# An mLSTM cell and a multiplicative feed-forward block on one core: four PSUM banks taken in another order, one product kept for the end, and unit 0's k and q loaded and turned ahead of the gates

## The chip, the core and the metric

The kernel runs on one NeuronCore of a Trainium2 chip. The metric is the device time of one execution in microseconds (us). A core has five engines that run their own queues in order: TensorE (PE, matrix products), VectorE (DVE), ScalarE (ACT), GpSimd (POOL) and SyncE (SP), which here only issues transfers. Sixteen DMA engines move the data.

## What is computed

Two blocks follow each other. The first is an mLSTM cell with stabilised exponential gates over 768 steps, for 4 batches of 8 heads with 40 channels. The second takes its output as 3072 tokens of 320 channels through a multiplicative feed-forward block:

```python
for t in range(S):
    m_new = np.maximum(f_gate[:, :, t] + m, i_gate[:, :, t])
    f_stab = np.exp(f_gate[:, :, t] + m - m_new)
    i_stab = np.exp(i_gate[:, :, t] - m_new)
    m = m_new
    C = f_stab * C + i_stab * outer(vt, kt)
    n = f_stab * n + i_stab * kt
    y[:, :, t] = sigmoid(o_gate) * (C @ qt) / np.maximum(np.abs(n @ qt), 1.0)
x = y.transpose(0, 2, 1, 3).reshape(B * S, H * D)
a = x @ w1; b = x @ w2            # 320 -> 1024
out = (a * b @ w3) @ w_out        # 1024 -> 1024 -> 320
```

The inputs q, k, v and the gates are float32, the four weights double precision (two 32-bit words each).

## The kernel before, in words

The sequence is cut into 24 units (`NU`): unit n is 128 time steps of one batch with its 8 heads, taken as two chunks of 64. The cell is computed in chunks, with matrix products within a chunk and a state carried between chunks. The feed-forward block works on six groups of four units. Since (ab w3) w_out = ab (w3 w_out), the kernel first forms `w3o` = w3 w_out (the `wp` products) and then needs per group only a, b, their product `ab` and `po` = ab w3o.

A main loop of 32 steps (lines 709 to 802) interleaves everything. In step s the loop issues the loads of unit s+2 (`load` at line 125: k, q, v, and `load_o`), weighs v of unit s on GpSimd, turns k and q of unit s on TensorE and copies them out on ScalarE (`turn`, up to unit 9), runs the cell products of units s and s-1 (`quarter_work`), and as many feed-forward products as the lists `n_up`, `n_seven` and `n_down` say. Two weight pieces or so are made float32 in each of the first steps (`convert`: ScalarE scales the high words, VectorE does four passes). The matmuls stand on TensorE in exactly the order in which they are written, by a chain of dependences (`in_order`, line 84). Ahead of the loop stands a front: loads in a fixed order (lines 459 to 474), the gates, the masks of unit 0, and the first two conversions.

*Gates.* The gates lie as 96 rows by 256 columns, a third of the sequence for each of 32 heads. Line 514 scans f into F (running sums in chunks of 64), line 517 scans the maximum into U, line 519 carries the running maximum M over the chunks; `before` is M ahead of each chunk. From these come U (minus the stabilised maximum, relative) and a, which is needed with tokens on partitions: `gate_cols` transposes it on TensorE (`pg`) and ScalarE copies it to aT. VectorE forms U in three passes, GpSimd forms a in two beside it. `dec` and `pick` become the decay of the state, `w` the weights of v (wT), and `weights(0)` makes the masks of unit 0: TensorE spreads U over the partitions (`ub`), ScalarE takes eight exps into `pw`, GpSimd clears what lies above the diagonal.

*PSUM.* There are eight banks. Four belong to the pool `ps_m`, handed out in rotation by `mps` (line 77), and four to the two cell tiles. When the cell is finished (after step 24, line 781), the cell tiles are closed and a pool `ps_x` of four banks takes their place. `mps` keeps a list `banks` of pools, takes the first and puts it at the end, so that with two pools in the list the tiles come from them in turn.

*Groups 3 to 5.* They are done with seven products in place of eight (`up_by_seven`, Strassen's scheme in Winograd's form), one piece per step in steps 19 to 30. A piece has four parts: `shared` (p15 and p67: 16 matmuls as the trace counts, named p there), `single` (pa, pb), `left` (the last rows of x, then VectorE's sums into a_sb and ab) and `product` (VectorE, line 676: ab times a_sb). Between `shared` and `single`, after step 24, stands a `po` product of an earlier group (`ffn_out`, line 680: 8 products over f, 16 matmuls in the trace; ScalarE copies the result to o_sb and sends it out). The last step, 31, runs four such products, of the group that step 30 finished. The eight f of one such product need all pieces of the group.

Of the kernel before, what the change touches and what calls it, by code (L numbers as in the profile page):

```python
# [10 lines left out]
AF = mybir.ActivationFunctionType  # L11
OP = mybir.AluOpType
# [4 lines left out]
def kernel(  # L17
# [26 lines left out]
    nc = tc.nc  # L44

    B, H, S, D = q.shape
    L = 64
# [25 lines left out]
    banks = [ps_m]  # L73
# [28 lines left out]
    NB, NBQ = 4, 3  # L102
# [19 lines left out]
        c, b = divmod(n, B)  # L122
        return src[b, :, c * P:(c + 1) * P, :].rearrange("h p d -> p h d")

    def load(n):
        for dst, src in ((kbuf[n % NB][:, :, 0:D], k), (qbuf[n % NBQ][:, :, 0:D], q), (vbuf[n % NB][:, :, 0:D], v)):
            if src is not q or n < N_DVE:
                nc.sync.dma_start(out=dst, in_=rows(src, n))  # L128

# [73 lines left out]
    def fetch(kind, i, part):  # L203

        if kind == "w12":
            c0 = part * CW
            if i < 2 * KF:
                wt, src = ((w1, w1_d), (w2, w2_d))[i // KF]
                ko = i % KF
                dst, pieces = wt[:, ko, c0:c0 + CW], [(every, src[ko * 128:(ko + 1) * 128, cols(c0, CW)])]  # L210
            else:
                dst, pieces = wr[:, c0:c0 + CW], [(slice(j * REM, (j + 1) * REM), src[KF * P:DM, cols(c0, CW)])
                                                  for j, src in enumerate((w1_d, w2_d))]
        elif kind == "wo":
            dst, pieces = wo[:, i, :], [(square, wo_d[j * CQ + i * 32:j * CQ + (i + 1) * 32, :])
                                        for j, square in enumerate(squares)]
        else:
            dst, pieces = None, [(square, w3_d[i * 128 + part * 64:i * 128 + (part + 1) * 64, cols(j * CQ, CQ)]
                                  .rearrange("(m r) n -> r m n", m=2)) for j, square in enumerate(squares)]
        pend.append((dst, raw_tile(dst.shape[-1] if dst is not None else CW, pieces), i, part))  # L220
# [5 lines left out]
    def scale_next():  # L226
        scaled.append(pend.pop(0))
        scale(scaled[-1][1])
# [56 lines left out]
    def turn(n):  # L285


        if n >= N_DVE:
            for src, dst, name in zip(turned_in[n % 2], (kT_t, qT_t), ("kT", "qT")):
                dst[n] = sb.tile([128, NP, P], FP, name=name, tag=name)  # L290
                done = nc.vector.transpose(out=dst[n].rearrange("i p (r f) -> i p f r", f=4),
                                           in_=src[:, 32:TB].rearrange("i (p f d) -> i p f d", p=NP, f=4)[:, :, :, 0:32])
            return done
        for src, dst, name in ((kbuf[n % NB], kT_t, "kT"), (qbuf[n % NBQ], qT_t, "qT")):
            pt = mps([128, NP, P], "pt")
            for p in range(NP):
                transpose(pt[:, p, :], src[:, 2 * p:2 * p + 2, :].rearrange("p a b -> p (a b)"))
            dst[n] = sb.tile([128, NP, P], FP, name=name, tag=name)
            nc.scalar.copy(out=dst[n], in_=pt)  # L299
# [162 lines left out]
        nc.scalar.dma_start(out=a[r], in_=i_gate.rearrange("b h s -> (b h) s")[:, cs])  # L462

    w3o_words = w3o.rearrange("p f d -> p (f d)").bitcast(U32).rearrange("p (n two) -> p n two", two=2)
    fetch("w12", 0, 0)
    fetch("w12", 1, 0)
    load(0)
    load_o(0)
    fetch("w12", 2, 0)
    idle += [w3o_words[:, i * CW:(i + 1) * CW] for i in range(2)]  # L470
# [39 lines left out]
    V = nc.vector  # L510
# [10 lines left out]
        if i + 1 < GR:  # L521
            V.tensor_copy(out=M[third[i + 1], 0:1], in_=M[r, GC:GC + 1])
    before = M[:, 0:GC].unsqueeze(2).to_broadcast([RG, GC, L])
    V.tensor_tensor(out=U3, in0=U3, in1=before, op=OP.subtract)
    nc.gpsimd.tensor_tensor(out=a3, in0=a3, in1=before, op=OP.subtract)
    V.tensor_tensor(out=U, in0=U, in1=F, op=OP.max)
    nc.gpsimd.tensor_tensor(out=a, in0=a, in1=F, op=OP.subtract)
    V.tensor_tensor(out=U, in0=F, in1=U, op=OP.subtract)
    for i, r in enumerate(third):
        nc.sync.dma_start(out=U_d[i * GC:(i + 1) * GC].rearrange("c r t -> r c t"), in_=U3[r])  # L530
    def gate_cols(src, dst, copy):
        pg = mps([P, GC // 2, GR, BH], "pg")
        for c in range(GC // 2):
            transpose(pg[:, c].rearrange("p g r -> p (g r)"), src[:, c * P:(c + 1) * P], RG)
        for c in range(GC // 2):
            copy(out=dst.rearrange("p (g c) r -> p c g r", g=GR)[:, c], in_=pg[:, c])

    scale_next()
    nc.scalar.activation(out=dec, in_=U3[:, :, L - 1], func=AF.Exp)
    gate_cols(a, aT, nc.scalar.copy)  # L540
    V.tensor_tensor(out=w3d, in0=a3, in1=U3[:, :, L - 1:L].to_broadcast([RG, GC, L]), op=OP.add)
    scale_next()
    convert()
# [6 lines left out]
    pd = mps([P, B * NP * NT], "pd")  # L550
    for x in range(2):
        mm(pd[halves[x]], odd[:, x].to_broadcast([RG, L]), pick.rearrange("p j g c -> p (j g c)"))
    turn(0)
    gate_cols(w, wT, nc.scalar.copy)
    nc.scalar.copy(out=decay.rearrange("p j c -> p (j c)"), in_=pd)
    nc.scalar.activation(out=g, in_=U, func=AF.Exp)
# [141 lines left out]
    sevens = [(gr, f) for gr in range(3, NG) for f in range(FH)]  # L698
    n_up = [0] * 4 + [1] * 2 + [2] * 11 + [0] * 15
    n_seven = [0] * 19 + [1] * 12 + [0]  # L700
    n_down = [0] * 17 + [2] * 6 + [1] * 8 + [4]
    w12 = [("w12", i, part) for part in range(2) for i in range(2 * KF + 1)]
    todo = w12[KF * 2 + 1:] + [("wo", i, 0) for i in range(FO)] + [("w3", ko, part) for ko in range(FO) for part in range(2)]
    n_cvt = [2, 1, 1, 1, 2, 2, 3, 3, 3] + [2] * 7
# [4 lines left out]
    for s in range(len(n_up)):  # L709
        if B <= s + 3 < NU:  # L710
            load_u(s + 3)
        if s + 2 < NU:
            load(s + 2)
            load_o(s + 2)
        if 0 < s < B - 1:
            weights(s + 1)
            out_gate(s)
        if s < NU:
            weighted(s)
            if s >= B:  # L720
                decayed(state[s % B][1], state[s % B][0], s, 0)
            if 0 < s < N_DVE:
                turn(s)
        if NY <= s - 2 < NU:
            send(s - 2)
        elif 0 <= s - 2 < NY:
            twice(s - 2)
        if NY <= s - 2 < NU:
            get_back(s - 2)
        while turned < min(s - 2, NY):  # L730
            x_trans(turned)
            turned += 1
        fold()
        seven = None
        if n_seven[s]:
            seven = up_by_seven(*sevens.pop(0), (lambda i: cell[i // 2][:, i % 2].rearrange("p (i t) -> p i t", i=2)) if s <= NU else
                                lambda i: mps([128, 2, TH], "p67" if i < 2 else "p15"))
            if s <= NU:
                seven[0]()
            seven[1]()  # L740
        if seven and s <= NU:
            ffn_out([downs.pop(0) for _ in range(n_down[s])], [cell[1][:, i, 0:DM] for i in range(2)])
        else:
            for _ in range(n_down[s]):
                ffn_out([downs.pop(0)])
        if seven and s > NU:
            seven[0]()
        now = [ups.pop(0) for _ in range(n_up[s])]
        open_ups = [up(*x) for x in now]
        if len(now) == 1 and turned == s - 2 < NY:  # L750
            x_trans(turned)
            turned += 1

        def rest():
            for x in open_ups:
                up_rest(*x)
            if seven:
                seven[2]()

        gated = None  # L760
        if s <= NU:
            gated = quarter_work(s, rest)
        else:
            rest()
        with tc.issue_after(gated.ins) if gated else nullcontext():
            if seven:
                seven[3]()
            if NY <= s - 2 < NU:
                x_turn(s - 2)
            if N_DVE <= s + 1 < NU:  # L770
                gated = turn(s + 1)
            if s in (16, 17):
                weight_sums(s - 16)
            if s - 2 in range(4 * GT - 1, NU, GT):
                token_sums((s - 2) // GT)
        if s == 0:
            gate_cols(g, gT, nc.scalar.copy)
            out_gate(0)
            scale_next()
            weights(1)  # L780
        if s == NU:
            cell_psum.close()
            banks.append(ctx.enter_context(tc.tile_pool(name="ps_x", bufs=4, space=bass.MemoryType.PSUM)))
        if B - 1 <= s < NU:
            if s + 1 < NU:
                weights(s + 1)
            out_gate(s)
        with tc.issue_after(gated.ins) if N_DVE <= s + 1 < NU else nullcontext():
            for _ in range(n_cvt[s] if s < len(n_cvt) else 0):
                convert()  # L790
                converted += 1
        if s >= ahead:
            while pend and len(scaled) < 2:
                scale_next()
        if N_DVE <= s + 2 < NU:
            load_turned(s + 2)
        while todo and fetched < converted + (2 if s < 2 else 3 if s < ahead - 1 else 4):
            fetch(*todo.pop(0))
            fetched += 1
        if s + 1 == pinned:  # L800
            for ins in keep_order(front):
                behind.enter_context(tc.issue_after(ins))
# [30 lines left out]
```

## Time and profile before

Three runs took 451.50, 451.76 and 454.91 us; the median is 451.76. The profiled execution took 451.65 us with a span of 449.8 us and a mean granted TensorE clock of 0.984.

| what | value |
|---|---|
| TensorE busy | 428.3 us, 95% of the span |
| VectorE busy | 342.5 us, 76% |
| ScalarE, GpSimd busy | 134.5 us (30%), 84.1 us (19%) |
| moved by DMA | 52.71 MB, 117 GB/s over the span |
| chain that ended last | TensorE 75%, DMA 8%, SyncE's issue 8%, VectorE 4% |
| L92 pa from xT, w: 240 matmuls | 62.3 us |
| L92 po from w3o, ab: 224 matmuls | 62.2 us |
| L309 idle of GpSimd before it | 183.2 us |

How to read it: a row of the profile names the source line, the engine, the operation, what it writes and reads, how often it ran, and its busy time; behind it stands how long the engine stood idle just before and what ended the wait. A line can be that of a helper: every matmul has line 92 and every transpose line 95, so they are told apart by their tiles. The busy share of TensorE is an average: its matmuls overlap, and the chain of waits tells better where the time is set. Idle time of an engine that is not the bottleneck costs nothing, such as GpSimd's above.

### The profile page before, as it was taken

What the parts mean: (1) busy time and instruction counts of PE and PEld (TensorE: products, weight loads), DVE (VectorE), ACT (ScalarE), POOL (GpSimd) and SP (SyncE); (2) the same over time, 40 slices, a digit from 0 to 9 for tenths busy, and PEclk for the clock granted to TensorE, in tenths of its full rate; (3) what the DMA queues carried; (4) which work ended last, traced back from release to release, by engine and by line L of the source; (5) the groups of instructions that cost most, each with busy time, mean ns of one, the idle gap of its engine ahead of it and who ended that gap; (6) DMA issues with size and microseconds to landing.
All of it is one profiled execution on the core that took longest, in us unless ns stands there. A gap on an engine that the chain in (4) does not pass through costs nothing.

```text
span 449.8 us, 12909 instructions
## 1 busy us (share of the span) xinstructions
PE 428.3 (95%) x5271; PEld 339.4 (75%) x5271; DVE 342.5 (76%) x703; ACT 134.5 (30%) x376; POOL 84.1 (19%) x156
## 2 busy tenths in 40 slices
PE   2998989999999999999999999999999899999997
PEld 2887778787778878887877877878777677777764
DVE  6699599999998988898868859759698856444530
ACT  3754454434533244133302320312210111101100
POOL 5353133333211220222022203202100000000000
PEclk9995899999999999999999999999999999999999
DMA  8999979797979786687466467264121110000001
GB/s 184 186 166 185 201 156 172 138 197 172 202 188 204 156 172 164 162 163 148 97 111 141 106 133 148 72 131 101 42 50 33 38 32 17 15 16 15 16 15 44
DMA packets 136554, 52.71 MB, mean 117 GB/s; under 512 B 109936, under 2 KB 127536, under 8 KB 136496
## 3 DMA queue, kind: packets, MB, share of 16 engines
q1 hardware_dynamic: 132896, 47.87, 53.1%
q10 hardware_dynamic: 3600, 4.03, 2.6%
q8 instruction: 41, 0.67, 0.7%
q14 instruction: 17, 0.14, 0.1%
HBM read 46.07 MB, written 5.80 MB: 115 GB/s over the span
## 4 chain that ended last, share of the span: by engine, by line
PE 75%; DMA 8%; SPq 8%; DVE 4%; issue 2%; ACT 1%; POOL 0%; DVEq 0%; ACTq 0%
PE cell L92 21%; PE pa L92 16%; PE po L92 13%; PE pb L92 10%; PE wp L92 7%; PE p L92 5%; SPq L173 4%; DMA kbuf<-in_k_dram 3%; DMA raw<-in_moe_w_dram 2%; DMA raw<-in_moe_w_out_dram 2%; SPq L128 2%; DMA q_all<-in_q_dram 1%; PE pt L95 1%; SPq L137 1%; PE px L95 1%
## 5 line engine op out<-in xcount | busy, mean ns | idle before, releaser
L92 PE MATMUL pa<-xT,w 128*128 128x256 f32 x240 | 62.3, 392 | 0.8 <-ACT xT L440 0.8
L92 PE MATMUL po<-w3o,ab 128*128 128x320 f32 x224 | 62.2, 434 | 0.8 <-DVE ab L676 0.8
L92 PEld LDWEIGHTS po<-w3o,ab 128*128 128x128 f32 x224 | 42.4, 190 | 18.2 <-DVE ab L676 1.3
L309 POOL TENSOR_TENSOR state<-state,decay 128x164 f32<-128x164 f32 x40 | 19.7, 492 | 183.2 <-DVE den L390 180.8
L92 PEld LDWEIGHTS pa<-xT,w 128*128 128x128 f32 x240 | 45.7, 195 | 9.1 <-ACT xT L440 1.6
L92 PE MATMUL pb<-xT,w 128*128 128x256 f32 x192 | 45.6, 381 | 0.8 <-ACT kT L299 0.8
L633 DVE SCALAR_TENSOR_TENSOR a_sb<-pa,wo 128x512 f32<-128x512 f32 x12 | 8.3, 692 | 48.9 <-PE pa L92 48.9
L282 POOL TENSOR_SCALAR_AFFINE_SELECT pw<-pw 64x512 f32<-64x512 f32 x48 | 35.0, 729 | 52.6 <-ACT pw L280 51.0
L92 PE MATMUL cell<-w3o,ab 128*128 128x320 f32 x160 | 44.0, 432 | 0.0
L92 PEld LDWEIGHTS pb<-xT,w 128*128 128x128 f32 x192 | 36.6, 191 | 6.4 <-ACT kT L299 1.5
L280 ACT ACTIVATE pw<-pw,aT 128x64 f32<-128x64 f32 x160 | 40.3, 336 | 2.9 <-ACT o_sb L688 2.9
L92 PEld LDWEIGHTS cell<-w3o,ab 128*128 128x128 f32 x160 | 30.5, 190 | 12.0
L585 ACT ACTIVATE a_sb<-pa 128x512 f32<-128x512 f32 x24 | 14.3, 597 | 76.8 <-PE pb L92 76.8
L92 PE MATMUL pa<-xT,wr 64*64 64x256 f32 x384 | 36.8, 386 | 0.0
L92 PE MATMUL wp<-wo,w3T 128*128 128x320 f32 x128 | 35.9, 433 | 0.5 <-DVE ab L586 0.5
L92 PE MATMUL pb<-xT,wr 64*64 64x256 f32 x384 | 36.2, 380 | 0.0
L382 DVE TENSOR_TENSOR h<-cell,h 64x164 f32<-64x164 f32 x96 | 31.2, 325 | 1.8
L92 PEld LDWEIGHTS wp<-wo,w3T 128*128 128x128 f32 x128 | 23.7, 190 | 9.6 <-DVE ab L586 0.7
L92 PEld LDWEIGHTS pa<-xT,wr 64*64 64x64 f32 x384 | 19.0, 133 | 14.4 <-issue 8.4
L688 ACT COPY o_sb<-po 128x320 f32<-128x320 f32 x14 | 6.0, 425 | 68.4 <-PE po L92 64.5
L586 DVE TENSOR_TENSOR ab<-pb,a_sb 128x512 f32<-128x512 f32 x24 | 16.1, 686 | 12.2 <-ACT a_sb L585 12.2
L178 ACT ACTIVATE raw<-raw 128x512 f32<-128x512 f32 (+1 forms) x32 | 19.1, 627 | 12.4 <-DMA raw<-in_moe_w_dram 11.2
(124 smaller groups left out, 749.8 us busy)
## 6 DMA issues: line engine op xcount, KB each, us to landing
raw<-in_moe_w_dram SPq DMA_DIRECT2D x64, 128.0 KB, 3.1
pw<-U_d SPq DMA_DIRECT2D x40, 128.0 KB, 4.1
kbuf<-in_k_dram SPq DMA_DIRECT2D x24, 160.0 KB, 4.3
vbuf<-in_v_dram SPq DMA_DIRECT2D x24, 160.0 KB, 4.9
o_in<-in_o_gate_dram SPq DMA_DIRECT2D x24, 160.0 KB, 4.4
out_dram<-o_sb ACTq DMA_DIRECT2D x24, 160.0 KB, 1.8
raw<-in_moe_w_dram SPq DMA_DIRECT2D x7, 512.0 KB, 6.3
raw<-in_moe_w_out_dram SPq DMA_DIRECT2D x32, 80.0 KB, 2.5
```

The lines of the kernel that those rows point to most:

```text
L92: in_order(nc.tensor.matmul(out, lhsT=lhsT, rhs=rhs, start=start, stop=stop))
L95: in_order(nc.tensor.transpose(out, in_, ident[0:n, 0:n]))
L128: nc.sync.dma_start(out=dst, in_=rows(src, n))
L173: nc.sync.dma_start(out=dst, in_=src)
L178: nc.scalar.activation(out=hi, in_=hi, func=AF.Prelu, scale=2.0 ** -111, alpha=2.0 ** 32)
L280: nc.scalar.activation(out=pw[:, h, :], in_=src[:, h, :], func=AF.Exp, bias=aT[:, c, b * H + h:b * H + h + 1])
L282: nc.gpsimd.affine_select(out=pw[r], in_=pw[r], compare_op=OP.is_ge, fill=0.0, base=0, pattern=[[0, H], [1, L]], channel_multiplier=-1)
L309: nc.gpsimd.tensor_tensor(out=new, in0=old, op=OP.mult, in1=decay[:, b * NP:(b + 1) * NP, 2 * c + x:2 * c + x + 1] .to_broadcast([P, NP, D1]))
L382: nc.vector.tensor_tensor(out=part, in0=ph[x][halves[e]], in1=part, op=OP.add)
L585: nc.scalar.mul(out=a_sb, in_=pa, mul=UP ** -2)
L586: nc.vector.tensor_tensor(out=ab_t[gr][j][:, fs[0]:fs[-1] + 1, t0:t0 + a_sb.shape[-1]], in0=pb, in1=a_sb, op=OP.mult)
L633: nc.vector.scalar_tensor_tensor(out=out, in0=p, scalar=UP ** -2, in1=q, op0=OP.mult, op1=OP.add)
```

## The change

There are three parts. First, after the cell's banks are given back, the list of pools is filled so that four tiles in a row come from the old pool and the next four from the new one, so that the products that follow at once do not ask for a bank in which the cell was just read. Second, step 30 runs no `po` product and step 31 runs five, so that one product whose inputs are long ready stands ahead of the four that need VectorE's last pass. Third, at the front: k and q of unit 0 are called for ahead of all weights, v after the first weight block; they are turned ahead of the gates' transposes; ScalarE's first two scalings of weights move behind `dec`; and VectorE alone forms a and U, in four passes, with the carried maximum added to F instead of taken from both.

```diff
-    def load(n):
-        for dst, src in ((kbuf[n % NB][:, :, 0:D], k), (qbuf[n % NBQ][:, :, 0:D], q), (vbuf[n % NB][:, :, 0:D], v)):
+    def load(n, which=slice(0, 3)):
+        for dst, src in ((kbuf[n % NB][:, :, 0:D], k), (qbuf[n % NBQ][:, :, 0:D], q), (vbuf[n % NB][:, :, 0:D], v))[which]:
...
+    load(0, slice(0, 2))
     fetch("w12", 0, 0)
+    load(0, slice(2, 3))
     fetch("w12", 1, 0)
-    load(0)
     load_o(0)
     fetch("w12", 2, 0)
...
-    V.tensor_tensor(out=U3, in0=U3, in1=before, op=OP.subtract)
-    nc.gpsimd.tensor_tensor(out=a3, in0=a3, in1=before, op=OP.subtract)
-    V.tensor_tensor(out=U, in0=U, in1=F, op=OP.max)
-    nc.gpsimd.tensor_tensor(out=a, in0=a, in1=F, op=OP.subtract)
-    V.tensor_tensor(out=U, in0=F, in1=U, op=OP.subtract)
+    V.tensor_tensor(out=F3, in0=F3, in1=before, op=OP.add)
+    V.tensor_tensor(out=a, in0=a, in1=F, op=OP.subtract)
+    V.tensor_tensor(out=f_sb, in0=F, in1=U, op=OP.min)
+    V.tensor_tensor(out=U, in0=f_sb, in1=U, op=OP.subtract)
...
+    turn(0)
+    gate_cols(a, aT, nc.scalar.copy)
+    nc.scalar.activation(out=dec, in_=U3[:, :, L - 1], func=AF.Exp)
     scale_next()
-    nc.scalar.activation(out=dec, in_=U3[:, :, L - 1], func=AF.Exp)
-    gate_cols(a, aT, nc.scalar.copy)
     V.tensor_tensor(out=w3d, in0=a3, in1=U3[:, :, L - 1:L].to_broadcast([RG, GC, L]), op=OP.add)
     scale_next()
     convert()
...
-    turn(0)
     gate_cols(w, wT, nc.scalar.copy)
...
-    n_down = [0] * 17 + [2] * 6 + [1] * 8 + [4]
+    n_down = [0] * 17 + [2] * 6 + [1] * 7 + [0, 5]
...
-            banks.append(ctx.enter_context(tc.tile_pool(name="ps_x", bufs=4, space=bass.MemoryType.PSUM)))
+            banks.extend([ps_m] * 3 + [ctx.enter_context(tc.tile_pool(name="ps_x", bufs=4, space=bass.MemoryType.PSUM))] * 4)
```

## The prediction

> **What bounds the kernel now.** I read the page first: TensorE is busy 95% of the span and 75% of the chain of waits is its own, so only TensorE's idle time can be won. The chain in order of time says where that is. From 122.25 us on it is TensorE almost without a break, so I looked there for the breaks; ahead of 122 it runs through DMA, issue and VectorE, so there I asked what ends each wait. There are three places.
>
> First, where the four cell banks are given back (step 25). The time lines of TensorE and VectorE:
>
> ```profile
> 351.35 0.70 PE L92 MATMUL p<-xT,w 128*128 128x256 f32 x2
> 351.89 0.59 PE L92 MATMUL p<-w3T,raw 128*128 128x256 f32 x2
> 354.38 0.67 PE L92 MATMUL p<-xT,w 128*128 128x256 f32 x2 [1.90 <-DVE h L382]
> 357.05 4.47 PE L92 MATMUL po<-w3o,ab 128*128 128x320 f32 x16
> ...
> 350.56 0.69 DVE L633 SCALAR_TENSOR_TENSOR a_sb<-pb,wo 128x512 f32<-128x512 f32 x1 [0.17 <-PE pb L92]
> 351.77 0.68 DVE L631 TENSOR_TENSOR ab<-pb,wo 128x512 f32<-128x512 f32 x1
> 352.37 0.49 DVE L377 TENSOR_TENSOR h<-cell,gT 128x328 f32<-128x328 f32 x1
> 352.89 1.34 DVE L382 TENSOR_TENSOR h<-cell,h 64x164 f32<-64x164 f32 x4
> ```
>
> The first p (a bank of the old pool) is written at 351.35; the second (a bank of the new pool, which lies where the cells were) waits for the last of the four h additions, until 354.38.
>
> Second, the end:
>
> ```profile
> 428.10 1.88 PE L92 MATMUL po<-w3o,ab 128*128 128x320 f32 x6
> 430.76 15.88 PE L92 MATMUL po<-w3o,ab 128*128 128x320 f32 x58 [0.78 <-DVE ab L676]
> ...
> 427.36 0.69 DVE L633 SCALAR_TENSOR_TENSOR a_sb<-pa,wo 128x512 f32<-128x512 f32 x1 [5.44 <-PE pa L92]
> 430.02 1.28 DVE L676 TENSOR_TENSOR ab<-ab,a_sb 128x512 f32<-128x512 f32 x2
> ```
>
> The first of the four last products runs six of its sixteen matmuls and then stands until VectorE has formed the last ab.
>
> Third, the front. Lines of the chain, and of TensorE and ScalarE:
>
> ```profile
> 11.67 9.25 DMA kbuf<-in_k_dram
> 29.52 6.18 DMA q_all<-in_q_dram
> 36.55 5.75 DMA kbuf<-in_k_dram
> ...
> 20.97 1.11 PE L95 MATMUL pt<-ident,kbuf 128*128 128x128 f32 x4 [0.29 <-DMA kbuf<-in_k_dram]
> 35.83 1.09 PE L95 MATMUL pt<-ident,q_all 128*128 128x128 f32 x4 [0.26 <-DMA q_all<-in_q_dram]
> 45.79 3.78 PE L92 MATMUL pa<-xT,w 128*128 128x256 f32 x8 [0.57 <-ACT xT L440]
> ...
> 6.24 0.66 ACT L178 ACTIVATE raw<-raw 128x512 f32<-128x512 f32 x1 [2.73 <-DMA raw<-in_moe_w_dram]
> 9.18 0.68 ACT L178 ACTIVATE raw<-raw 128x512 f32<-128x512 f32 x1
> 12.77 0.59 ACT L299 COPY kT<-pt 128x512 f32<-128x512 f32 x1
> ```
>
> k of unit 1 lands at 20.92, q of unit 3 at 35.7, k of unit 4 at 42.3, and TensorE turns each at once: up to 45.8 us transfers pace the front, not the gates or unit 0. By stretches of time the 16 DMA engines are full from 4 us on, but for a dip at 22 to 24.
>
> **What the Trainium skill says.** "TensorE: Matmul & The Clock Gate", Part 1, has the array at half clock until it was busy for about a 3.4 us window, which runs free of the kernel. The trace agrees: granted 0.50 up to 49, 0.77 in 49 to 50, 1.00 after, so about 3.7 us after the dense pa began at 45.79; 32 cell matmuls (cell from vw, kbuf) took 1.09 us at 15.46 and 0.63 at 53.87. (The record's 1.00 ahead of 34 us contradicts the 1.09; I take the durations.) "DMA: Bandwidth & Descriptors", Specifications, wants 512 B per piece for line rate; rows of q, k, v, o are 160 B. The trace: 360 GB/s in 5.5 to 6 us with weights in flight, 117 to 155 in 8 to 9.5 us with k and q. "PSUM — Partial Sum Buffer", Specifications: eight banks per partition, which is four in the old pool and four in the cells; no run here counts them.
>
> **The change part by part.**
>
> *Banks.* Before, old and new pool alternate, so step 25's p tiles are old, new, old, new. After, its four are all old: the banks that held pa, pb, pa, pb of step 24. VectorE reads these last, ending 350.39, 351.25, 351.85 and 352.45. TensorE wants them at 351.35, then after one p each: 16 matmuls in 3.65 us (chain, each later step) is 0.91 per p, so about 352.3, 353.2, 354.1. None waits, and the 1.90 us go. The wait could reappear at po, now the first in a new bank: it is wanted at 351.35 + 3.75 = 355.1, and the cells are free at 354.25. It passes, by 0.85. VectorE is not pushed: its queue is unchanged, full to 360.6, and the next pa it wants falls at 363.2. The transposed y of the last unit, issued back at 359.12 to 362.2 and some 2.5 us in landing, is wanted at 367.1. Both hold. Later both rotations reuse a bank after eight tiles, so the period of 12.43 us stays. Gain 1.9.
>
> *Product kept back.* Step 30 loses one po (4.31 us); step 31 runs it first. pa of step 30 then comes 4.31 earlier, at 423.05 on the old clock. VectorE is through with step 30's sums at 421.9 (1.28 us of ab from 417.59, then 3.1 us of sums), so it can follow, with 1.1 to spare. Its chain from pa to the first finished ab is 430.67 - 427.36 = 3.3 us, so 426.4. TensorE ends the upward part at 423.8, runs the kept product to 428.1 and needs that ab at 429.7: no wait. What is won is the stall: four products take 4 x 4.31 = 17.24 us; from 428.10, with the 0.19 that ScalarE's copy trails in a step without a wait (411.29 - 406.79 - 4.31), the last copy would start at 445.53. It started at 446.68. Gain 1.15.
>
> *Gates by VectorE.* Two GpSimd passes (0.84 + 0.79) go; VectorE has four passes in place of three. Before, they took 0.42, 0.72 and 0.83, the slow two with GpSimd beside them; four of 0.42 plus 0.04 between end at 6.49 + 1.85 = 8.34 against 8.53. a is ready at 7.4 against 8.25. Both feed unit 0 alone.
>
> *k and q of unit 0 first, turned first.* In the record by tile they landed at 3.13 + 6.1 = 9.2 and 3.60 + 6.7 = 10.3. Issued at 2.2 and 2.7 ahead of all weights, with 164 KB at about 150 GB/s each and 1.4 us to land, I estimate 5.5 and 6.6. TensorE turns them at half clock (1.1 us each), done at 7.7; ScalarE copies (0.59 each) by 8.4, so a's transposes, now behind them in TensorE's queue, start at 7.7 instead of 8.30. That removes 1.2 us of ScalarE copies between the masks' exps and wT. Against this, both weight scalings now stand ahead of the gate's exp in ScalarE's queue, and the second weight block lands behind k, q, the first block and v. Summing the same bytes, I estimate 10.8 (range 9.5 to 11.5). Then scaling 0.66, gate exp 0.41, eight mask exps 1.75, wT: 13.9 against 14.5; the masks reach GpSimd at 13.7 instead of 12.77, and behind its two selects (1.8) is vw, so vw comes at 16.3 against 15.4. Behind the waiting scaling stand thus the gate exp, the masks, GpSimd's vw and TensorE's state matmul. At 9.5 it would be 0.3 early instead. So unit 0 moves by -0.3 to +1.2, likely +0.8.
>
> Neither reaches the end. Until k of unit 1 was called (11.67), the same set of transfers is issued in another order through full engines, so I leave 20.92, 35.7 and 42.3 where they are. Early work waits there; late work is taken up by TensorE's waits at 33.4 to 42.4 (0.49, 0.56, 0.26, 0.43, 0.54). VectorE, later by as much, has 5.19 us idle ahead of its ab at 53.34. The up products' start, and with it the clock's release, stay. Front: 0, bounds -1.2 and +1.7 (one clock window of 3.4 us at half rate).
>
> Sum: 1.90 + 1.15 + 0 = 3.05; 451.76 - 3.05 = 448.7.
>
> **Rivals.**
>
> *The front gains too (447.5).* If unit 0, not the transfers, paces the front, the 1.2 us of copies off ScalarE's path come through. For it: TensorE waited a mere 0.29 for k of unit 1. Against: later waits end with transfers as well.
>
> *The front gives back (450.4).* The scaling that waits in ScalarE's queue holds unit 0, and the up products slip past a clock window: +1.7. For it: the release came 3.7 us after the dense work began, nearly the least possible. Against: up starts on a transfer that the change doesn't move.
>
> *Slower (453.8).* That +1.7, with 1.5 of unit 0's delay not taken up, and the bank wait merely moved to po, as the margin is 0.85: -1.15 + 3.2 = +2.05. It needs three slips at once.
>
> **How the numbers follow.** Forecast 0.56; front gains 0.18; front gives back 0.17; slower 0.09. The range from 446.8 to 451.2 holds the first three with the front's bounds and some 0.7 us of spread between runs (451.5 and 451.76, the third being 454.91). Faster by over 1% means below 447.2: the far half of the second case and a little of the first, 0.18. Slower by over 1% (456.3) is a tail of the last, 0.05. The rest, 0.77.
>
> **What would show it.** Banks: no wait on h among the p matmuls near 351, and po straight behind. Product: 80 po matmuls at the end in one run with no idle, VectorE's last ab done before the second of the five begins. Front: k and q of unit 0 landed before 7.5, the second scaling on ScalarE waiting for its transfer, but k of unit 1 at 20.9 and the first dense pa near 45.8. I am wrong if pa starts over 0.7 us off that, or if po waits at the bank change.

## The result and the profile after

The changed kernel took 447.16 us (median of six runs, 445.75 to 448.17). In the same session the kernel before took 453.24 (451.50 to 456.95), so the ratio is 0.986, with a 95% interval from 0.981 to 0.990. Against the forecast of 448.7 it is 1.5 us lower. The profiled execution took 445.75 us, the fastest of the six, with a span of 444.0, which is 5.8 below the span of before, 449.8. Three fixed points on TensorE split that difference:

| stretch | before | after | gained | forecast |
|---|---|---|---|---|
| start to the first p of step 25 | 351.35 | 348.73 | 2.62 | 0 |
| from there to po, the bank change | 5.70 | 3.56 | 2.14 | 1.90 |
| from po to the first p of step 30 | 58.61 | 58.61 | 0 | 0 |
| from there to ScalarE's last copy | 31.02 | 29.97 | 1.05 | 1.15 |

The two late parts came in within 0.25 us of the forecast. What was missed is the front. Its row is of this one pair of runs, though: in two later traces of the changed kernel the first p of step 25 starts at 351.43 (*e5_again*) and 349.38 (*e13_all*), so 2.62 is not yet what the front is worth. Here is the bank change in the time lines of TensorE and VectorE of the kernel after (start, duration, engine, line, what it writes and reads, how many, idle time before it):

```profile
348.73 0.70 PE L92 MATMUL p<-xT,w 128*128 128x256 f32 x2
349.26 0.59 PE L92 MATMUL p<-w3T,raw 128*128 128x256 f32 x2
349.69 0.59 PE L92 MATMUL p<-xT,w 128*128 128x256 f32 x2
350.13 2.32 PE L92 MATMUL p<-w3T,raw 128*128 128x256 f32 x10
352.29 4.47 PE L92 MATMUL po<-w3o,ab 128*128 128x320 f32 x16
...
350.26 1.35 DVE L382 TENSOR_TENSOR h<-cell,h 64x164 f32<-64x164 f32 x4
```

No p waits for h any more. The reads of the cells end at 351.61 and po, the first product in a bank of theirs, starts at 352.29: a margin of 0.68, where 0.85 was forecast. The end:

```profile
418.06 1.04 PE L92 MATMUL pb<-xT,wr 64*64 64x256 f32 x16
419.03 21.80 PE L92 MATMUL po<-w3o,ab 128*128 128x320 f32 x80
...
418.29 0.69 DVE L633 SCALAR_TENSOR_TENSOR a_sb<-pa,wo 128x512 f32<-128x512 f32 x1 [1.14 <-PE pa L92]
419.15 0.69 DVE L633 SCALAR_TENSOR_TENSOR a_sb<-pb,wo 128x512 f32<-128x512 f32 x1 [0.17 <-PE pb L92]
419.76 0.68 DVE L631 TENSOR_TENSOR ab<-pa,wo 128x512 f32<-128x512 f32 x1
420.36 0.68 DVE L631 TENSOR_TENSOR ab<-pb,wo 128x512 f32<-128x512 f32 x1
420.96 1.28 DVE L676 TENSOR_TENSOR ab<-ab,a_sb 128x512 f32<-128x512 f32 x2
```

All 80 matmuls of the five last products run in one piece. VectorE waited 1.14 us for pa, the slack of 1.1 that the forecast gave it, and its last ab is there at 422.24, ahead of the second product at about 423.4 (419.03 plus a fifth of 21.8).

The front, in the order of the forecast's steps. ScalarE and GpSimd of the kernel after:

```profile
6.74 0.59 ACT L299 COPY kT<-pt 128x512 f32<-128x512 f32 x1 [3.25 <-PE pt L95]
8.81 0.66 ACT L178 ACTIVATE raw<-raw 128x512 f32<-128x512 f32 x1
10.47 0.68 ACT L178 ACTIVATE raw<-raw 128x512 f32<-128x512 f32 x1 [0.99 <-DMA raw<-in_moe_w_dram]
11.04 0.40 ACT L545 ACTIVATE gates<-gates 96x256 f32<-96x256 f32 x1
11.35 1.71 ACT L280 ACTIVATE pw<-ub,aT 128x64 f32<-128x64 f32 x8
12.92 0.40 ACT L536 COPY wT<-pg 128x96 f32<-128x96 f32 x2
...
15.27 0.73 POOL L304 TENSOR_TENSOR vw<-vbuf,wT 128x328 f32<-128x328 f32 x1
```

The second scaling waits for its block as forecast, the gate's exp and the masks stand behind it, and vw starts at 15.27 where it started at 14.67. So unit 0 is later, by 0.6 us. Yet the first dense products are earlier. TensorE's turning of k and q and the first dense pa:

```profile
5.62 1.09 PE L95 MATMUL pt<-ident,kbuf 128*128 128x128 f32 x4 [5.62 <-DMA kbuf<-in_k_dram]
6.84 1.09 PE L95 MATMUL pt<-ident,q_all 128*128 128x128 f32 x4
21.22 1.12 PE L95 MATMUL pt<-ident,kbuf 128*128 128x128 f32 x4
33.87 1.11 PE L95 MATMUL pt<-ident,kbuf 128*128 128x128 f32 x4
39.77 0.63 PE L95 MATMUL pt<-ident,kbuf 128*128 128x128 f32 x4 [0.21 <-DMA kbuf<-in_k_dram]
40.87 0.63 PE L95 MATMUL pt<-ident,q_all 128*128 128x128 f32 x4 [0.47 <-DMA q_all<-in_q_dram]
42.60 1.99 PE L92 MATMUL pa<-xT,w 128*128 128x256 f32 x8 [0.78 <-ACT xT L440]
```

k of unit 4 is turned at 39.77 (before 42.43), and pa starts 3.2 us ahead of the 45.8 that the forecast left in place. (It also takes 1.99 us in place of 3.78, since the granted clock was up already in this run; the last section comes back to that.) SyncE's queue says why the transfers came sooner. Here is its time line before, where each row is one issue, or several of a kind, with the time that SyncE spent in it. A transfer is *called* when its issue starts and has *landed* when its data is there:

```profile
2.19 0.90 SPq L173 DMA_DIRECT2D raw<-in_moe_w_dram  x2
3.13 0.43 SPq L128 DMA_DIRECT2D kbuf<-in_k_dram  x1
3.60 0.63 SPq L128 DMA_DIRECT2D q_all<-in_q_dram  x1
4.28 3.41 SPq L128 DMA_DIRECT2D vbuf<-in_v_dram  x1
...
11.67 0.67 SPq L128 DMA_DIRECT2D kbuf<-in_k_dram  x1
```

and after:

```profile
2.18 0.43 SPq L128 DMA_DIRECT2D kbuf<-in_k_dram  x1
2.65 0.58 SPq L128 DMA_DIRECT2D q_all<-in_q_dram  x1
3.28 0.84 SPq L173 DMA_DIRECT2D raw<-in_moe_w_dram  x1
4.16 0.43 SPq L128 DMA_DIRECT2D vbuf<-in_v_dram  x1
...
9.74 0.65 SPq L128 DMA_DIRECT2D kbuf<-in_k_dram  x1
```

Before, the issue of v of unit 0, the third transfer of 160-byte rows behind two weight blocks of 512 KB, held SyncE for 3.41 us. After, it took 0.43. Part of that comes back in later issues (that of the third weight block took 2.16 in place of 1.14), and k of unit 1 is called at 9.74 in place of 11.67. The stretches of time agree. Their last three columns are the granted clock, the DMA engines' busy share and GB/s, before and then after:

```profile
8.00:12.00 4.00, 3.70 (x40) 2.75 (x41) 3.67 (x8) 2.56 (x11) 1.98 (x4) 1.00 1.21 180
```

```profile
8.00:12.00 4.00, 3.56 (x40) 2.38 (x38) 2.79 (x7) 3.01 (x11) 0.92 (x3) 1.00 1.09 317
```

In both the engines count as full, but they move 180 GB/s in one and 317 in the other. The two stretches don't hold the same transfers (v and the output gate of unit 0 were issued at 4.3 to 8.5 us before, at 4.2 to 5.7 after), so the sum from the start is the fairer comparison. With the two stretches of 4 us ahead of these (95 and 280 GB/s before, 69 and 254 after), the first 12 us moved 4 x (95 + 280 + 180) = 2.22 MB before and 4 x (69 + 254 + 317) = 2.56 MB after. The lead of 0.34 MB at the 180 GB/s of that stretch is 1.9 us, as much as the lead with which unit 1 is called; by 24 us it is 4.26 MB against 4.63.

### The profile page after: what moved, and what is told of

Same layout as the page of the kernel before. It is cut to its first block, busy times and chain, and to the rows that moved or that the text cites. A ratio compares the mean times of both kernels' runs of the same rounds, so it can differ in the third digit from the quotient of the medians.

```text
span 444.0 us, 12907 instructions
## 1 busy us (share of the span) xinstructions
PE 420.7 (95%) x5271; PEld 332.6 (75%) x5271; DVE 342.8 (77%) x704; ACT 133.8 (30%) x376; POOL 81.7 (18%) x154
## 4 chain that ended last, share of the span: by engine, by line
PE 75%; DVE 8%; SPq 6%; DMA 4%; issue 2%; POOL 2%; ACT 1%; DVEq 0%; ACTq 0%; POOLq 0%
PE cell L92 22%; PE pa L92 17%; PE po L92 14%; PE pb L92 11%; PE wp L92 7%; PE p L92 5%; SPq L173 3%; DMA raw<-in_moe_w_dram 2%; DMA raw<-in_moe_w_out_dram 1%; DVE h L382 1%; DMA o_in<-in_o_gate_dram 1%; DVE pw L355 1%; DVE ex L189 1%; SPq L137 1%; DVE ma L191 1%
## 5 line engine op out<-in xcount | busy, mean ns | idle before, releaser
L92 PE MATMUL pa<-xT,w 128*128 128x256 f32 x240 | 60.5, 383 | 0.9 <-ACT xT L440 0.8
L92 PEld LDWEIGHTS pa<-xT,w 128*128 128x128 f32 x240 | 44.5, 190 | 8.6 <-ACT xT L440 1.5
L92 PE MATMUL cell<-vw,kbuf 64*64 64x41 f32 x704 | 16.4, 227 | 6.6 <-POOL vw L304 4.4
```

The source lines that it names most:

```text
L92: in_order(nc.tensor.matmul(out, lhsT=lhsT, rhs=rhs, start=start, stop=stop))
```

## The experiments

There are three groups. The first takes the change apart. The second tests, on the changed kernel, what could hold or use the front's gain. The third runs the two halves of the front crosswise on top of the late parts. In the table, "loads" is the new order of the first transfers, "gates" the four VectorE passes with the early turning and the moved scalings, "late" the banks and the product kept back. The three last columns are from the one profiled run of each kernel, which need not be its median run. Each ratio is to the kernel before on the same chip, as recorded; it is not the quotient of the medians shown.

| kernel | loads | gates | late | median us (runs) | ratio, 95% interval | k of unit 1 called | first dense pa | first p of step 25 |
|---|---|---|---|---|---|---|---|---|
| before | | | | 452.15 to 453.24 | 1 | 11.67 | 45.79 | 351.35 |
| after | x | x | x | 447.16 (6) | 0.986, 0.981 to 0.990 | 9.74 | 42.60 | 348.73 |
| e1_tail | | | x | 448.83 (9) | 0.993, 0.991 to 0.996 | 11.89 | 45.34 | 352.40 |
| e2_loads | x | | | 451.35 (14) | 0.999, 0.997 to 1.001 | 9.48 | 43.51 | 348.83 |
| e3_gates | | x | | 452.45 (22) | 1.000, 0.998 to 1.003 | 11.60 | 45.13 | 353.07 |
| e4_grouped | grouped | x | x | 447.14 (6) | 0.991, 0.987 to 0.994 | 9.00 | 42.98 | 349.61 |
| e5_again | x | x | x | 446.96 (6) | 0.986, 0.983 to 0.990 | 10.64 | 44.48 | 351.43 |
| e6_scale | x | x, scaling later | x | 447.19 (6) | 0.987, 0.983 to 0.990 | 10.26 | 44.45 | 350.61 |
| e7_ahead | x | x | x, fetching ahead | 447.99 (6) | 0.988, 0.984 to 0.992 | 10.86 | 45.48 | 352.01 |
| e8_w0_first | one block first | | | 451.89 (1) | | 10.30 | 45.99 | 351.62 |
| e10_late | | | x | 448.37 (6) | 0.991, 0.988 to 0.994 | 11.70 | 45.66 | 352.27 |
| e11_late_loads | x | | x | 446.60 (6) | 0.987, 0.984 to 0.990 | 9.47 | 42.48 | 350.31 |
| e12_late_gates | | x | x | 448.94 (7) | 0.992, 0.989 to 0.995 | 11.89 | 46.90 | 352.96 |
| e13_all | x | x | x | 447.34 (6) | 0.988, 0.985 to 0.991 | 9.81 | 43.83 | 349.38 |

### The change taken apart

*e1_tail* is the kernel before with the two late edits alone:

```diff
-    n_down = [0] * 17 + [2] * 6 + [1] * 8 + [4]
+    n_down = [0] * 17 + [2] * 6 + [1] * 7 + [0, 5]
...
-            banks.append(ctx.enter_context(tc.tile_pool(name="ps_x", bufs=4, space=bass.MemoryType.PSUM)))
+            banks.extend([ps_m] * 3 + [ctx.enter_context(tc.tile_pool(name="ps_x", bufs=4, space=bass.MemoryType.PSUM))] * 4)
```

> The kernel before with the two late parts alone: four banks of the old pool first, one product kept back. The front is as before. In the profiles of before and after the stretch from the first p at the bank change to po shrank from 5.70 to 3.56 us, and the stretch from step 30's p to the last copy from 31.02 to 29.97. Both theories of the front expect that here too: 2.14 + 1.05 = 3.2 us less, about 450 us against 453.2. The rest of after's gain, about 2.9 us of the medians, is then the front's. If this kernel alone gains the whole 6 us, the front does nothing and the rest was spread between runs.

Measured: 448.83, a ratio of 0.993, which is 3.1 us of 452 (interval 2.0 to 4.2). The forecast sum for the late parts, 3.05, stands.

*e2_loads* is the kernel before with the new order of the first transfers alone:

```diff
+    load(0, slice(0, 2))
     fetch("w12", 0, 0)
+    load(0, slice(2, 3))
     fetch("w12", 1, 0)
-    load(0)
     load_o(0)
```

> The kernel before with the order of the first transfers alone: k and q of unit 0 first, then the first weight block, v, the second block, the output gate. Gates, turning and scalings as before. Theory T (the order of transfers moves data sooner: small rows run beside 4 KB weight rows): k of unit 1 is called for about 9.7 and lands about 18 us, as in after, not 11.67 and 20.9; k of unit 4 is called about 34 and the first dense pa starts near 43; 2 to 3.5 us less than before. Rival G (the gates, the turning and the scalings do it): called and landed as before, 11.7 and 20.9, pa near 45.8, no gain. Rival C (only the moment of the clock's release differs from run to run): the transfers as before, and a time within 1 us of before.

(The argument `which` of `load` is added as in the whole change.) Measured: k of unit 1 is called at 9.48 and the first pa starts at 43.51, so the transfers come sooner by the order alone, which rival C denied. The time, 451.35, has an interval from 1.6 us of gain to 0.3 of loss: too close to nothing to say whether it gains, and less than the 2 to 3.5 us that theory T gave for it.

*e3_gates* is the rest of the front, without the order of loads:

```diff
-    load(0, slice(0, 2))
     fetch("w12", 0, 0)
-    load(0, slice(2, 3))
     fetch("w12", 1, 0)
+    load(0)
     load_o(0)
```

(shown against the kernel after, with the late edits taken back as well).

> The other half of the front alone: turning ahead of the gates, scalings behind dec, a and U by VectorE, with the transfers in the order of before, and neither of the late parts. k of unit 0 now lands at about 9.2, so the turning holds the gates' transposes until about 11.4. Theory T: k of unit 1 still called about 11.7 and landing about 20.9; unit 0 is 2 to 3 us late, TensorE stands for the up products as before or later: 0 to 3 us slower. Rival G: 2 to 3 us faster than before. Rival C: within 1 us of before.

Measured: 452.45, ratio 1.000, with an interval of about 1 us to either side. The gates by VectorE and the early turning, by themselves, are worth nothing that can be measured.

*e4_grouped* is the kernel after with all four transfers of unit 0 ahead of the weights, to see whether small and large rows have to be mixed:

```diff
-    load(0, slice(0, 2))
-    fetch("w12", 0, 0)
-    load(0, slice(2, 3))
-    fetch("w12", 1, 0)
+    load(0)
     load_o(0)
+    fetch("w12", 0, 0)
+    fetch("w12", 1, 0)
     fetch("w12", 2, 0)
```

> The changed kernel with one thing altered: k, q, v and output gate of unit 0 all ahead of the first three weight blocks, so that small and large rows are no longer mixed. If mixing is what makes the transfers faster (theory T, mixing): 656 KB of small rows alone at 150 to 200 GB/s up to about 7.5 us, the weights after it, k of unit 1 called nearer 11 than 9.7, 1 to 2 us slower than after; the first weight blocks land later and so hold ScalarE's queue too. If it is only that the small rows stand ahead (their issue isn't held behind a full queue): called near 9.7 or sooner and no slower than after but for ScalarE's wait, about 1 us.

Measured: k of unit 1 is called at 9.00, sooner still, and the issue of v took 0.86 us. The median, 447.14, is 1.7 us under that of e1_tail on the same chip. Whether it is quite as fast as the kernel after stays open: the ratios, 0.991 and 0.986, are from two sessions, and their intervals overlap. So the mixing isn't needed for the early call; it is enough that the small rows aren't issued behind large blocks. *e8_w0_first* is the kernel before with one weight block ahead of k, q and v in place of two:

```diff
     fetch("w12", 0, 0)
-    fetch("w12", 1, 0)
     load(0)
+    fetch("w12", 1, 0)
     load_o(0)
```

> The kernel before with the first weight block still first, then k, q, v of unit 0, the second block, the output gate. One look, for the times of the transfers. If it is the two weight blocks at the head that hold up the rest (v's issue stood 3.41 us behind them), one block at the head costs half: k of unit 1 called near 10.6, between 11.67 (two ahead) and 9.48 (none ahead). If any weights ahead of k and q cost all of it: near 11.7. If only the second block's place matters: near 9.5.

```profile
3.76 2.52 SPq L128 DMA_DIRECT2D vbuf<-in_v_dram  x1
6.33 0.76 SPq L173 DMA_DIRECT2D raw<-in_moe_w_dram  x1
...
10.30 0.69 SPq L128 DMA_DIRECT2D kbuf<-in_k_dram  x1
```

In its SyncE time line v's issue holds SyncE for 2.52 us behind one block. Over all traces it is 3.22 to 4.16 behind two blocks (five traces) and 0.43 to 0.86 in the two orders that start with small rows (eight traces). k of unit 1 is called at 10.30. That is sooner than with two blocks ahead (11.60 to 11.89), but no later than in the three kernels on the same chip that start with small rows (10.26 to 10.86, e5_again to e7_ahead): there the third weight block's issue held SyncE longer instead (2.71 and 2.78 in e6_scale and e5_again). So one block ahead makes v's issue long, but that it delays the call of unit 1 isn't shown. Its single time tells nothing.

### What holds the front after the change

*e5_again* is the kernel after, run beside the next two.

> The changed kernel itself, beside the next two on the same chip. Expected 4.5 to 5.5 us less than before. The late parts alone gave 0.9932 of the time before; what is under that is the front's, expected 1.2 to 2 us.

It took 446.96, like the first time, but in its profiled run (448.42, the slowest of the six) the first pa started at 44.48 and not at 42.60, and at step 25 nothing of the front's lead is left: the first p starts at 351.43, in the kernel before at 351.35. One place where it was lost is a wait for kT:

```profile
78.33 3.46 PE L92 MATMUL pb<-xT,w 128*128 128x256 f32 x8 [2.67 <-ACT kT L299]
```

Behind the wait of 2.67 us these eight matmuls take 3.46 us in place of the 1.99 of the kernel after (76.26), and the granted clock reads 0.50 from 78 to 81 us. So besides the wait about 1.5 us more went there.

*e6_scale* moves the second weight scaling behind the copies of wT, out of the way of the gate's exp and the masks:

```diff
     V.tensor_tensor(out=w3d, in0=a3, in1=U3[:, :, L - 1:L].to_broadcast([RG, GC, L]), op=OP.add)
-    scale_next()
     convert()
...
     gate_cols(w, wT, nc.scalar.copy)
+    scale_next()
```

> The changed kernel with the second weight scaling moved on ScalarE from ahead of the gate's exp to behind the copies into wT. In the profile of after it waits 0.99 us for its transfer and runs 0.68, and the gate exp, the masks' exps, GpSimd's selects and vw stand behind it. Theory V (after the transfers came sooner, unit 0 and then VectorE's full queue, from the masking at 17.32 to the first ab at 49.37 with 0.73 us idle, set the up products' place): vw 1.2 us earlier (about 14.1), VectorE's masking about 16.1, and the kernel 0.5 to 1.2 us faster than after. Theory D (transfers alone set the front): vw earlier by as much, no change in time (within 0.3 us).

GpSimd and VectorE of this kernel:

```profile
13.69 0.78 POOL L304 TENSOR_TENSOR vw<-vbuf,wT 128x328 f32<-128x328 f32 x1
...
16.13 0.68 DVE L355 TENSOR_TENSOR pw<-cell,pw 128x512 f32<-128x512 f32 x1
```

vw comes 1.58 us earlier than after the change (13.69 against 15.27) and VectorE's masking 1.19 (16.13 against 17.32), yet the time stays: 447.19 against 446.96. The traces agree: k of unit 1 is turned 1.43 us sooner than in e5_again (19.74 against 21.17), k of unit 4 no sooner (41.25 against 41.32). So unit 0's lateness, which the change brought, costs nothing that can be measured. Six runs of each fix the difference only to about 1 us to either side, worked out from their spread; by the time alone, most of theory V's 0.5 to 1.2 us isn't excluded.

*e7_ahead* goes after a wait by which the kernel after loses part of its lead. ScalarE scales w_out pieces there as they land, and kT's copy stands behind them in its queue (the time lines of ScalarE and TensorE, kernel after):

```profile
74.37 0.49 ACT L178 ACTIVATE raw<-raw 128x320 f32<-128x320 f32 x1 [1.27 <-DMA raw<-in_moe_w_out_dram]
75.25 0.50 ACT L178 ACTIVATE raw<-raw 128x320 f32<-128x320 f32 x1 [0.39 <-DMA raw<-in_moe_w_out_dram]
75.64 0.56 ACT L299 COPY kT<-pt 128x512 f32<-128x512 f32 x1
...
76.26 1.99 PE L92 MATMUL pb<-xT,w 128*128 128x256 f32 x8 [1.55 <-ACT kT L299]
```

TensorE's pb waits 1.55 us for kT. The edit has the weight pieces called further ahead from step 4 on:

```diff
-        while todo and fetched < converted + (2 if s < 2 else 3 if s < ahead - 1 else 4):
+        while todo and fetched < converted + (2 if s < 2 else 3 if s < 4 else 4):
```

> The changed kernel with weight pieces fetched up to four ahead from step 4 on, where it was three up to step 7. In after ScalarE stands 1.27 and 0.39 us near 74 for w_out pieces, the copies of kT stand behind that in its queue, and TensorE's pb waits 1.5 us for them: of 3.97 us by which after led at the first ab, 2.63 are left from 120 us on. Theory B (that wait gives the lead back): the wait at 74 is gone, the start of the po run near 225.4 falls about 1.3 us earlier, and so does the end. Rival S (SyncE's queue is in order, so a piece called for earlier waits for VectorE to free its buffer and holds the loads behind it): the wait moves, and the time is the same or up to 2 us worse.

Measured: 447.99, no gain. In its ScalarE time line the same copy of kT still waits, and one step earlier a scaling waits that had not waited so long:

```profile
66.36 0.49 ACT L178 ACTIVATE raw<-raw 128x320 f32<-128x320 f32 x1 [2.88 <-DVE den L392]
...
78.48 0.49 ACT L178 ACTIVATE raw<-raw 128x320 f32<-128x320 f32 x1 [1.81 <-DMA raw<-in_moe_w_out_dram]
78.88 0.57 ACT L299 COPY kT<-pt 128x512 f32<-128x512 f32 x1
```

TensorE stands 1.59 us for that kT (1.55 in the kernel after), and 1.06 us at 67.38 for the kT of the step before, behind the scaling at 66.36, whose wait the profile puts down to VectorE, as rival S said. So here calling for more at once did not take the wait away and added one. It is one trace, and the wait is not the same in each: e13_all, which is the kernel after, has none at this copy and one of 1.68 us at 103.12.

### Loads and gates crosswise

The first group left half of the front's gain without an owner: the whole change was about 2 us below the late parts, loads alone showed 0.8, gates alone nothing. Either loads carry all of it, or the two only work together. Four kernels on one chip decide: late parts alone (*e10_late*, the edit of e1_tail), with loads (*e11_late_loads*, the edits of e1_tail and e2_loads), with gates (*e12_late_gates*, the kernel after with the edit shown at e3_gates), with both (*e13_all*, the kernel after).

> Before plus the two late parts alone, now the base line for three others on the same chip: with the new order of loads, with the new gates and turning, with both. Late parts forecast 3.05 us, seen 3.2 in traces: ratio to before 0.993. Every theory agrees on this one.

> Late parts and the new order of the first transfers, old gates and turning. If the order of loads carries the whole of the front's gain (theory T), this equals the whole change: 2 us below the late parts alone, ratio to before about 0.9875. If loads and turning only help together (theory J), it stays within 1 us of the late parts alone, ratio 0.991 to 0.993.

> Late parts with the new gates, the early turning and the moved scalings, old order of loads. Both T and J say that this gains nothing over the late parts: ratio to before about 0.993. If the gates gain by themselves (theory G), it is 1 us or more below the late parts, ratio 0.990 or less.

> The whole change once more, as the fourth corner. 446.9 to 447.2 earlier, ratio 0.986: some 2 us below the late parts alone. Under T the gap between this and late parts with loads is under 0.5 us; under J it is 1 us or more.

Measured, as medians: loads take 448.37 to 446.60 (1.77 less) without the gates, and 448.94 to 447.34 (1.60 less) with them. From the means of the runs the effect of loads is -1.8, with about 0.7 to either side at 95%, worked out from the spread of the four kernels' runs (standard errors of 0.37, 0.21, 0.48 and 0.20; the mean of two differences then has 0.34). The gates have +0.6 and +0.7 by medians, +0.5 by means: nothing, or a little worse. Thus loads carry the whole of what is seen here and the joint effect isn't needed. The 0.7 us of gain by the ratio of e2_loads, from 1.6 of gain to 0.3 of loss, is smaller, but its interval overlaps with this one. TensorE of e10_late, then of e11_late_loads, at unit 4's k and at the first p of step 25:

```profile
42.48 1.11 PE L95 MATMUL pt<-ident,kbuf 128*128 128x128 f32 x4
...
352.27 0.70 PE L92 MATMUL p<-xT,w 128*128 128x256 f32 x2
```

```profile
39.62 0.63 PE L95 MATMUL pt<-ident,kbuf 128*128 128x128 f32 x4 [1.76 <-DMA kbuf<-in_k_dram]
...
350.31 0.70 PE L92 MATMUL p<-xT,w 128*128 128x256 f32 x2
```

The lead is 2.86 us at unit 4 and 1.96 at step 25, and the wait for k shows that transfers still pace the front where they come sooner. But the one lead is not simply what is left of the other. At VectorE's first ab it was 0.45 (51.41 against 50.96), since the first pa ran at full clock in e10_late (1.99 us) and at half in e11_late_loads (3.78). Then e10_late waited 1.93 us for kT at 78.69, and the sixteen matmuls behind that wait took 1.7 us longer than the same ones in the kernel after (2.81 and 2.80 against 1.99 and 1.89). A single pair of traces therefore can't size the front. All traces together point the same way as the times: the first p of step 25 stands at 351.35 to 353.07 in the five with the old order (mean 352.4; e8_w0_first left out) and at 348.73 to 352.01 in the eight with small rows first (mean 350.1).

## Why the forecast was near, and where it failed

*Banks: right.* 2.14 for 1.90. The wait went and did not move to po, with 0.68 of margin. The forecast took the idle time of one row, 1.90; the whole stretch from p to po, 5.70, set against the same stretch of a step without a wait (415.66 to 419.22 before, 3.56) would have given 2.14. It also put 3.75 where that step has 3.56, hence a margin of 0.85.

*Product kept back: right.* 1.05 for 1.15, and VectorE had the 1.1 us to spare that were worked out. Both parts together: 3.05 forecast, 3.2 in the profiled run, 3.1 (2.0 to 4.2) in e1_tail and 4.3 (2.9 to 5.6) in e10_late.

*Gates by VectorE: right.* The passes took 0.42, 0.42, 0.41 and 0.42 and ended at 8.07, for 8.34 forecast.

*k, q first and unit 0: right.* k landed at 2.18 + 3.3 = 5.5 and q by 6.84, for 5.5 and 6.6 (with some luck: the terms given for k, 2.2, then 164 KB at 150 GB/s, then 1.4 to land, sum to 4.7); the second block landed by 10.47 for 10.8; vw's start moved by +0.6, for +0.8. e6_scale takes that delay away and gains nothing that can be measured, so it is hidden, as the forecast had it.

*Front, 0: wrong.* The step that failed is "the same set of transfers is issued in another order through full engines, so I leave 20.92, 35.7 and 42.3 where they are". That the set is the same and the engines are full does not fix when it is through: full engines moved 180 GB/s between 8 and 12 us in one order and 317 in the other, and SyncE, which has to issue one transfer before it comes to the next, stood 3.41 us in one of them. Both were to be seen before: the stretch at 8 to 12 us next to that at 4 to 8 (280 GB/s, as full), and a row of 3.41 us in the chain of waits in front of the very row, `11.67 9.25 DMA kbuf<-in_k_dram`, that the forecast quoted. Unit 1's k landed at 9.74 + 8.2 = 17.9, not 20.9; unit 4's was turned at 39.77, and pa started at 42.60, 3.2 us off, where over 0.7 was the forecast's own sign of being wrong. In the crosswise runs this term is worth 1.8 us. With the late parts' 3.2 (profiled run) to 4.3 (e10_late) that makes 5.0 to 6.1, for a measured gain of 6.4, 6.2 and 5.4 (the ratios 0.9858, 0.9864 and 0.9881 of three comparisons, on 452 to 453 us). That 447.16 lies only 1.5 under the forecast is luck of the base: 453.24 in that session, 451.76 in the forecast. Of the gain itself the forecast had half, 3.05.

That the early work would wait at unit 1 was half right: there TensorE took k up at 21.22, though it lay there since 17.9, since unit 0 was late. But units 3 and 4 took up the lead.

*The rival "the front gains too" (447.5)* came near in time, for another reason. Its 1.2 us were ScalarE's copies off unit 0's path; e11_late_loads keeps them on the path and is no slower than the whole change (446.60 against 447.34), and e6_scale frees unit 0 further for nothing that can be measured. "The front gives back" and "slower" did not come.

What stays open: why the same transfers run at a higher total rate when the small rows go first. What the long issue waits for is not shown either. The longest one stands in every trace, old order or new: v of unit 1 holds SyncE for 4.86 to 6.14 us (5.50 before, 4.90 after), and no run moved it. Nor was the lead's loss between the first dense products (3.97 us at VectorE's first ab, 49.37 against 53.34) and step 25 (2.62) followed to its end: waits on ScalarE's queue were shown, and e7_ahead did not win them back. And whether the order of loads is worth as much without the late parts as with them (0.7 against 1.8) the intervals don't settle.

## What to carry to other kernels

Where transfers pace a stretch, take from the profile both how full the engines are and how many GB/s they move, and read the issuing queue's own time line: an issue that lasts microseconds postpones all that stands behind it. Here it paid to issue the short-row transfers that are wanted early ahead of the large blocks, and a reordering of "the same bytes" has to be priced, not set to zero. The waits at the change of buffers and at the very end were forecast to within 0.25 us from the rows around them, with the margin of the next wait in line. An effect of 2 us at the front can't be sized from one trace of each kernel: three traces of one kernel had step 25 at 348.73, 349.38 and 351.43.

## What the hardware showed that was not expected

A transfer of 160-byte rows (v of unit 0) held its issuing queue for 3.22 to 4.16 us behind two blocks of 512 KB, 2.52 behind one, and 0.43 to 0.86 where such rows went first.

Two of VectorE's passes over 96 x 256 took 0.72 and 0.83 us before, while GpSimd worked beside them; after, with GpSimd out of it, all four took 0.41 to 0.42. GpSimd's work is not shown to be the cause: the first pass of before took 0.42 too (6.49 to 6.91), although GpSimd's record (6.54 to 7.38) lies beside it.

The clock of TensorE came up at different moments in runs of one program. The first dense pa in the profiled run of the kernel after, and then in that of e13_all, which is the same kernel:

```profile
42.60 1.99 PE L92 MATMUL pa<-xT,w 128*128 128x256 f32 x8 [0.78 <-ACT xT L440]
```

```profile
43.83 3.78 PE L92 MATMUL pa<-xT,w 128*128 128x256 f32 x8 [0.57 <-ACT xT L440]
```

The first ran at the full clock from its start, the second at half. "TensorE: Matmul & The Clock Gate", Part 1, of the Trainium skill says that the monitor's window runs free of the kernel and that the number of slow matmuls at the start changes from run to run; these two lines agree, and put 1.8 us on it here. The forecast's "3.7 us after the dense work began" was therefore not a fixed step to build on, and its trace agreed with the window less than it said: in the kernel before TensorE was busy through all of 36 to 40 us at a granted 0.50, and the clock came up only at 49 to 50.

The clock also fell again in the middle of a run. TensorE waited 2.67 us for kT in e5_again and 1.93 in e10_late (at 78.33 and 78.69), and the granted clock read 0.50 at 78 to 81 and 80 to 83 us. Waits at the same place of 1.22 to 1.59 us in four other traces (after, e1_tail, e4_grouped, e7_ahead) were not followed by such a drop.
